# Last stage of an FNet and ReGLU layer: the second column half of B22 made with seven products of quarters, with the sums of weights prepared in the gate stage

## The chip, the cores and the metric

One NeuronCore of a Trainium2 chip runs the whole kernel in one launch. The metric is the device time of the launch in microseconds (us), lower is better; the time before is the median of three runs. Engines are named as in the profile: PE (matrix products), PEld (PE's weight loads), DVE (vector), ACT (scalar), POOL (general, here also a queue of transfers), SP (a queue of transfers).

## The reference

```python
xn = layernorm(x)                                  # x: 1 x 2048 x 640, fp32
a, b = xn @ dft_hid_re.T, xn @ dft_hid_im.T        # 640 x 640 each
mix = dft_seq_re @ a - dft_seq_im @ b              # 2048 x 2048 each
gate, up = xn @ W_gate, xn @ W_up                  # 640 x 1728 each
h = gate * (gate > 0) * up
out = x + mix + h @ W_down                         # W_down: 1728 x 640
```

## The kernel before

**Products in three parts.** All products are of fp32 values held as a rounded high part and a low part. `split` (L199 to L201) makes them: ACT copies the high part (L200), DVE subtracts it for the low part (L201). `mm3` (L202 to L208) makes one product of 128 x 128 weights and 128 x 512 values with three matmuls: high by high (L206), high by low (L207), low by high (L208).

**Stages.** The first stage (0 to about 405 us) does the sequence transform. The gate stage (406 to about 699 us) makes `gate`, `up` and `h` in 13 tiles of 128 columns of F. The last stage (700 us to the end) multiplies the hidden transform and `h` by `dft_hid` and `W_down`, and adds x. Both products of the last stage are one long sum over 12 pairs of blocks: five `hid` pairs from the transform, and seven pairs of tiles of `h`, the last of them odd (a tile and the 64 columns left over). Quads are two such pairs each.

**The gate stage.** A tile is a period of 33 units; a unit is a product of three matmuls, 0.68 us. What happens in a period stands in tables of numbers: products and sums in `STEPS`, the making of weight sums in `SUMS`, `WEIGHTS`, `SPLITS`. Each action is entered with a key, `at(key, f)`, and all are written out in the order of their keys; the engines run them in that order. Actions of a tile that this text speaks of: `seed` (ACT, L1102) copies one PSUM bank into another with a sign, `add_snap` (DVE, L1112) adds a kept copy to a bank, `add_out` (DVE, L1117) takes a bank out, `both` (DVE, L1123) makes a new bank of an old one and a kept one, once per tile, `final` (DVE, L1129) makes `h`. PSUM has eight banks, and a bank that such an action frees is what a later product starts in: the third `add_snap` of a tile after `both` frees the bank that ACT's seed then fills for PE's first product of the next tile. The weight sums `gw` (L1007) are placed by `plan_sums` on DVE or beside it on POOL, by due times; the `w`, `wa`, `wb` instructions (L1083) are the low parts of the sums.

**Tasks.** The gate stage also prepares weights of the last stage. A task has five steps, each with its own key: load on SP (tile `pl`), TASK_LEAD units ahead of the task's key; prepare on DVE (four small sums, `pw`); a rounding on ACT 1.2 units later; `rounded` on DVE (a subtraction of 512 or 384 columns) at the task's second key; the store on SP TASK_STORE later. `pair_half` tasks (24) make the sums for a pair of blocks and write them to `wparts`. `quad_weights` tasks (5) make the sums for a quad of blocks (L1306, L626, L1308, L626, and L1317 for `rounded`), and write to `wquads`. The 29 tasks stand three to a period from period 2, the last two in period 11. `plain_parts` copies go beside them on POOL.

**`grow`.** The products of quarters also need sums of the moving operand. `grow` builds them in memory with POOL's transfers from memory to memory, some of them accumulating: for each of three groups a chain of eight transfers (`grown`), 14 units apart; each link waits for the one it reads.

**The last stage.** `project(q)` runs for the sequence halves q = 1, then q = 0. For each it makes products of sums of halves named B11, T1, T2, B22, B21, T3, T4, over seven `UNITS`. Each unit has load, fetch (weights), prepare (`split`), run and read (additions to the output tile `y`, DVE, L1452 and L1454). B22 is the product that is treated on a second level, for column half 0: `second_level` replaces it with seven products of quarters, named 1256374, over three `GROUPS` (5 blocks in all) and both sequence halves at once. Four of the seven have a second product for an odd row block. Column half 1 of B22 is made straight. `QUADS_AFTER` says after which units of `project` the next of the 21 quarter units comes. `drive_last` runs each unit's load 0, fetch and prepare some steps ahead of its run: AHEAD 6, ROWS 6, READY 3. Weights have seven buffers (`wts`), the split operands four (`ring2`), the loaded operands 16 (`raws`). In this stage PE, SP and POOL are written out by hand, DVE and ACT are ordered by the scheduler.

Of the kernel before, what the change touches and what calls it, by code (L numbers as in the profile page):

```python
# [128 lines left out]
def fnet_reglu_kernel(  # L129
# [42 lines left out]
    wquads = dram_p.tile([P, len(QUADS), 4, 2 * P], F32, name="wquads")  # L172
    grown = [dram_p.tile([4, P, n, CH], F32, name=f"grown{g}") for g, (_, _, n, _) in enumerate(GROUPS)]
# [840 lines left out]
    def plan_sums():  # L1014
# [278 lines left out]
    def quad_weights(i):  # L1293
# [25 lines left out]
        def store():  # L1319
            nc.sync.dma_start(wquads[:, i], t["s"].rearrange("p s v n -> p s (v n)"))  # L1320
# [3 lines left out]
    tasks = [quad_weights(i) for i in range(len(QUADS))] + [pair_half(k, h) for k in range(NPAIR) for h in range(2)]  # L1324
    assert len(tasks) <= len(TASK_KEYS) * (NF - 3)
    for i, (load, prepare, round_, rounded, store) in enumerate(tasks):
        key, second = (PERIOD * (2 + i // len(TASK_KEYS)) + key for key in TASK_KEYS[i % len(TASK_KEYS)])
# [8 lines left out]
    def quarter(q, g, half):  # L1336
        what, k, n, _ = GROUPS[g]
        if what == "hid":
            return pqd[2 * q][1][:, k + half * n : k + half * n + n]
        first = 2 * (k + half * n) + 1  # L1340
        return hd[q][first : first + 2 * n - 1 : 2, :, :CH].rearrange("f p t -> p f t")

    def grow(g):

        t = [grown[g][i] for i in range(4)]
        put = lambda o, i: lambda: nc.gpsimd.dma_start(o, i)
        more = lambda o, i: lambda: nc.gpsimd.dma_start(o, i, accum_op=OP.add)
        return [put(t[0], quarter(1, g, 0)), put(t[2], quarter(0, g, 1)), more(t[0], quarter(0, g, 0)), more(t[2], quarter(0, g, 0)),
                put(t[1], t[0]), more(t[1], quarter(0, g, 1)), put(t[3], t[1]), more(t[3], quarter(1, g, 1))]
# [75 lines left out]
    Y_BEFORE = {(1, "T1", 6): "B11", (1, "T2", 1): "T1"}  # L1425
# [40 lines left out]
    def project(q):  # L1466
# [7 lines left out]
        def get(kind, u):  # L1474
# [5 lines left out]
            col, row = int(kind in ("B12", "B22")), int(kind in ("B21", "B22"))  # L1480
# [13 lines left out]
        def unit(name, u, first, last):  # L1494
# [7 lines left out]
            def load():  # L1502
# [8 lines left out]
                if q and name == "T2" and u in (1, 5):  # L1511
                    get("B21", SINGLE[u // 5])
# [24 lines left out]
            def prepare():  # L1537
# [3 lines left out]
                r = lambda kind: raws[kind, u]  # L1541
# [109 lines left out]
        for name, us in (("B11", every), ("T1", every), ("T2", every), ("B22", every[:4]), ("T3", every), ("B22", every[4:]), ("T4", every)):  # L1651
            for u in us:
                now = [(name, u, u == every[0], u == every[-1])]
# [14 lines left out]
    def second_level():  # L1668
# [132 lines left out]
```

## Time and profile before

| what | value |
|---|---|
| median of three runs | 1001.67 us (1001.63 to 1002.9) |
| profiled execution, whole | 1000.28 us |
| its span | 998.5 us |
| PE busy | 992.9 us, 99% (4393 matmuls) |
| DVE busy | 883.0 us, 88% |
| ACT busy | 525.7 us, 53% |
| POOL busy | 147.0 us, 15% |
| granted clock of PE | 1.00 |
| moved by transfers | 261.13 MB, mean 262 GB/s |

The time of the profiled execution is 1.8 us above its span, and the median of the runs 1.4 above that. A row of the timeline reads: start, duration (both us), engine, line, operation, output<-inputs, shape, and in brackets the idle time of the engine just before with what ended it. A row of the waits reads: who waited, for whom, us in total, times, the longest. A row of groups ends with count, busy us, mean ns, and the idle time before.

### The profile page before, as it was taken

To read this page: it belongs to the slowest core of one execution; us is meant where nothing else is said; L and a number is where in the kernel's file an instruction comes from. 1 tells how busy PE (TensorE), PEld (TensorE's weight loads), DVE (VectorE), ACT (ScalarE), POOL (GpSimd) and SP (SyncE) were. 2 spreads that over 40 slices of the span, in tenths; PEclk is the share of its full clock that TensorE was granted. 3 is DMA by queue.
4 is the path that set the end of the run, shared out by engine and by line. 5 is a ranking of instruction groups with operands and counts; after the bars stand their busy time and mean duration, and the time that the engine had idled before them with its cause. 6 is when DMAs were issued, how large, how long until landed. Compare 5 with 4: busy or idle time off the path is not lost.

```text
span 998.5 us, 13547 instructions
## 1 busy us (share of the span) xinstructions
PE 992.9 (99%) x4393; PEld 818.4 (82%) x4393; DVE 883.0 (88%) x1459; ACT 525.7 (53%) x832; POOL 147.0 (15%) x288
## 2 busy tenths in 40 slices
PE   9999999999999999999999999999999999999998
PEld 8888888888888888878888888888788888888887
DVE  7967999999889989998999999997788887689887
ACT  6664444333333555776666666666444354454452
POOL 2000000000000000024444544432100000000001
PEclk9999999999999999999999999999999999999999
DMA  8977895985947967827997998765698879999784
GB/s 323 322 262 262 261 328 171 342 332 183 408 157 252 361 203 247 289 74 195 276 268 239 259 267 259 207 185 160 202 400 304 261 243 344 312 314 322 230 275 163
DMA packets 183670, 261.13 MB, mean 262 GB/s; under 512 B 14944, under 2 KB 127200, under 8 KB 183504
## 3 DMA queue, kind: packets, MB, share of 16 engines
q1 hardware_dynamic: 147200, 208.82, 61.9%
q0 software_dynamic: 10944, 38.44, 13.0%
q10 hardware_dynamic: 25456, 13.01, 4.4%
q8 instruction: 34, 0.56, 0.2%
q14 instruction: 36, 0.29, 0.1%
HBM read 198.34 MB, written 75.94 MB: 275 GB/s over the span
## 4 chain that ended last, share of the span: by engine, by line
PE 95%; DVE 3%; issue 1%; DMA 1%; ACT 0%; SPq 0%; DVEq 0%; ACTq 0%
PE ps L207 30%; PE ps L206 30%; PE ps L208 30%; PE ps L584 3%; PE ps L613 1%; PE ps L1599 1%; DMA pl<-in_wd 1%; PE ps L185 1%; DVE ev L1117 1%; DVE ev L1129 0%; DVE w L1083 0%; DVE gw L1007 0%; DVE wt L201 0%; DVE ps L1112 0%; DVE pw L1282 0%
## 5 line engine op out<-in xcount | busy, mean ns | idle before, releaser
L208 PE MATMUL ps<-cb,wt 128*128 128x512 f32 (+1 forms) x389 | 151.0, 388 | 0.2 <-DVE wt L201 0.2
L207 PE MATMUL ps<-cb,wt 128*128 128x512 f32 (+1 forms) x389 | 151.0, 388 | 0.1
L206 PE MATMUL ps<-cb,wt 128*128 128x512 f32 (+1 forms) x389 | 150.9, 388 | 0.0
L200 ACT ACTIVATE cb<-rw 128x1024 fp32r<-128x1024 f32 (+1 forms) x91 | 86.5, 962 | 82.5 <-PE ps L208 47.7
L200 ACT ACTIVATE cb<-raw 128x1024 fp32r<-128x1024 f32 x64 | 67.7, 1060 | 103.7 <-PE ps L208 61.8
L201 DVE TENSOR_TENSOR cb<-rw,cb 128x1024 fp32r<-128x1024 f32 (+1 forms) x91 | 99.3, 1103 | 18.7 <-ACT cb L200 17.9
L207 PE MATMUL ps<-cb,xs_late 128*128 128x512 f32 x232 | 90.6, 390 | 0.0
L206 PE MATMUL ps<-cb,xs_late 128*128 128x512 f32 x232 | 90.3, 389 | 0.0
L208 PE MATMUL ps<-cb,xs_late 128*128 128x512 f32 x232 | 90.3, 389 | 0.0
L201 DVE TENSOR_TENSOR cb<-raw,cb 128x1024 fp32r<-128x1024 f32 x64 | 77.9, 1219 | 13.3 <-ACT cb L200 13.2
L1102 ACT ACTIVATE ps<-ps 128x512 f32<-128x512 f32 x104 | 59.2, 581 | 56.3 <-DVE ps L1112 37.2
L207 PE MATMUL ps<-cb,xs_early 128*128 128x512 f32 x226 | 88.0, 390 | 0.0
L206 PE MATMUL ps<-cb,xs_early 128*128 128x512 f32 x226 | 87.9, 389 | 0.0
L208 PE MATMUL ps<-cb,xs_early 128*128 128x512 f32 x226 | 87.9, 389 | 0.0
L197 ACT ACTIVATE ev<-ps 128x512 f32<-128x512 f32 x117 | 70.0, 598 | 33.4 <-PE ps L208 31.6
L207 PEld LDWEIGHTS ps<-cb,wt 128*128 128x128 f32 x389 | 73.0, 188 | 15.6 <-DVE cb L201 0.5
L208 PEld LDWEIGHTS ps<-cb,wt 128*128 128x128 f32 x389 | 73.0, 188 | 15.4 <-DVE wt L201 0.6
L206 PEld LDWEIGHTS ps<-cb,wt 128*128 128x128 f32 x389 | 73.0, 188 | 15.2
L1117 DVE TENSOR_TENSOR ev<-ps,ev 128x512 f32<-128x512 f32 x91 | 62.3, 685 | 11.3 <-PE ps L208 10.4
L200 ACT ACTIVATE wt<-wt 128x768 fp32r<-128x768 f32 (+5 forms) x60 | 38.3, 646 | 51.0 <-DMA wt<-wparts 49.5
L1007 POOL TENSOR_TENSOR gw<-gw 128x128 f32<-128x128 f32 x101 | 47.0, 465 | 95.4 <-DVE wa L1083 25.1
L200 ACT ACTIVATE cb<-tk 128x1024 fp32r<-128x1024 f32 x32 | 33.8, 1060 | 51.0 <-DVE tk L751 25.5
(250 smaller groups left out, 2309.4 us busy)
## 6 DMA issues: line engine op xcount, KB each, us to landing
raw<-in_dft SPq DMA_DIRECT2D x94, 512.0 KB, 6.7
wt<-wparts SPq DMA_DIRECT2D x74, 256.0 KB, 4.6
rw<-hd SPq DMA_DIRECT2D x27, 512.0 KB, 6.1
hd<-ev SPq DMA_DIRECT2D x45, 256.0 KB, 3.8
tok<-r ACTq DMA_DIRECT2D x24, 448.0 KB, 6.3
wt<-wparts SPq DMA_DIRECT2D x27, 384.0 KB, 5.2
rw<-pq SPq DMA_DIRECT2D x19, 512.0 KB, 5.9
wparts<-pw SPq DMA_DIRECT2D x24, 384.0 KB, 4.3
```

Source lines behind the costliest of these rows:

```text
L185: nc.tensor.matmul(ps[:, :P], warm, warm, start=True, stop=True)
L197: return nc.scalar.activation(o, i, AF.Copy)
L200: nc.scalar.activation(hi, src, AF.Copy)
L201: return nc.vector.tensor_tensor(lo, src, hi.bitcast(F32), op=OP.subtract)
L206: nc.tensor.matmul(ps, wh, mh, start=first, stop=False, skip_group_check=more)
L207: nc.tensor.matmul(ps, wh, ml, start=False, stop=False, skip_group_check=more)
L208: nc.tensor.matmul(ps, wl, mh, start=False, stop=last, skip_group_check=more)
L584: nc.tensor.matmul(E[0, key], xn_part(n * SG + j, d)[v == 1], b[:, int(v == 2), j], start=False, stop=n % NH == NH - 1 and (j, v) == (SG - ...
L613: nc.tensor.matmul(E[c, key], xn_part(j, d)[v == 1], b[c][0][:, int(v == 2), j], start=j == 0 and v == 0, stop=False)
L1007: return (engine or nc.vector).tensor_tensor(operand(n, o), operand(n, a), operand(n, b), op=OP.add if op == "+" else OP.subtract)
L1102: nc.scalar.activation(banks[n, x], banks[n, s], AF.Copy, scale=float(sign))
L1117: tt(t, banks[n, x], snaps[n, s], op=OP.add if op == "+" else OP.subtract)
```

## The change

The second level is now used for column half 1 too: `second_level(c)` is run for c = 0 and 1. `project` makes B22 straight only for the two units of `SINGLE` (a pair left over and the odd pair). Column half 1 needs its own sums of weights, so there are five more `quad_weights` tasks, which read `Z4` of `wparts` as `pair_half` tasks have stored it, and its own sums of operands, so `grow` runs twice, the second chain 7 units behind the first. The 34 tasks stand three in period 1, three in each of periods 2 to 10, and four in period 11. The load of a task is 12.2 units ahead instead of 13, and its store 2.2 after the second step instead of 2.8. The due times of `plan_sums` move by some units. The places of the quarter units, of SINGLE's and of the loads of `y` are given anew, and the pool of loaded operands is divided. In the last stage this gives five products (15 matmuls) fewer on PE, 20 more instructions on ACT, and 21 loads of quarters (`rq`) more on SP.

```diff
-TASK_STORE = 2.8
-TASK_LEAD, TASK_KEYS = 13.0, ((8.2, 12.4), (18.6, 22.4), (31.2, 33.1))
-LOAD_LEAD, LOADED, RAW_DUE = 46, 38, 8.5
+TASK_STORE = 2.2
+TASKS_FIRST, TASKS_LAST = ((13.9, 18.9), (21.5, 27.5), (31.2, 33.9)), ((6.0, 9.0), (13.9, 17.5), (22.4, 26.0), (28.2, 34.3))
+TASK_LEAD, TASK_KEYS = 12.2, ((8.2, 11.8), (18.6, 22.4), (30.2, 32.1))
+LOAD_LEAD, LOADED, RAW_DUE = 46, 38, 9.5
...
-                due[i] = min([split_at.get(o, 99.0) - 8, RAW_DUE if raw else 99.0] + [due_at(j) - 0.8 for j in reads.get(o, ())])
+                due[i] = min([split_at.get(o, 99.0) - 5, RAW_DUE if raw else 99.0] + [due_at(j) - 0.8 for j in reads.get(o, ())])
...
-    def quad_weights(i):
+    def quad_weights(i, c):
...
-                nc.sync.dma_start(z[:, j * 2 * P : (j + 1) * 2 * P], pair(k, 1)[1][0][:, : 2 * P])
+                nc.sync.dma_start(z[:, j * 2 * P : (j + 1) * 2 * P], wparts[:, k, Z4 : Z4 + 2 * P] if c else pair(k, 1)[1][0][:, : 2 * P])
...
-    tasks = [quad_weights(i) for i in range(len(QUADS))] + [pair_half(k, h) for k in range(NPAIR) for h in range(2)]
-    assert len(tasks) <= len(TASK_KEYS) * (NF - 3)
+    tasks = [quad_weights(i, 0) for i in range(len(QUADS))] + [pair_half(k, h) for k in range(NPAIR) for h in range(2)]
+    tasks += [quad_weights(i, 1) for i in range(len(QUADS))]
+    keys = {1: TASKS_FIRST, NF - 2: TASKS_LAST}
+    task_at = [(PERIOD * n + a, PERIOD * n + b) for n in range(1, NF - 1) for a, b in keys.get(n, TASK_KEYS)]
...
     for g, key in enumerate((60, 184, 300)):
-        for i, step in enumerate(grow(g)):
-            at(key + 14 * i, step)
+        for c in range(2):
+            for i, step in enumerate(grow(g, c)):
+                at(key + 14 * i + 7 * c, step)
...
-                       ("wts2", AHEAD - 4, "left"), ("raws", 16, "left"),
+                       ("wts2", AHEAD - 4, "left"), ("raws", 9, "left"), ("quad", 5, "left"), ("y3", 1, "left"),
...
-    SINGLE_AFTER = ((("B22", 4), ("B22", 5)), (("B22", 0), ("B22", 1)))
-    QUADS_AFTER = [(1, "B22", u) for u in every[3:]] + [(0, "B11", u) for u in every] + [(0, "T1", u) for u in every[:6]] + [(0, "B22", u) for u in every[:4]]
+    SINGLE_AFTER = ((("T3", 6), ("B22", 4)), (("B22", 2), ("B22", 4)))
+    QUADS_AT = {1: {'T3': (0, 1, 1, 1, 0, 1, 2), 'T4': (0, 2, 1, 1, 2, 1, 1)}, 0: {'B11': (2, 2, 3, 3, 2, 2, 1), 'T1': (1, 0, 0, 2, 0, 2, 1), 'T2': (1, 2, 1, 0, 1, 0, 0), 'B22': (0, 0, 2, 0, 0, 0, 0)}}
...
-        for name, us in (("B11", every), ("T1", every), ("T2", every), ("B22", every[:4]), ("T3", every), ("B22", every[4:]), ("T4", every)):
+        for name, us in (("B11", every), ("T1", every), ("T2", every), ("B22", SINGLE if q else SINGLE[:1]), ("T3", every), ("B22", () if q else SINGLE[1:]), ("T4", every)):
...
-    quads = second_level()
-    Y_AFTER = {(1, "T2", 5): ((4, 0),), (1, "T4", 5): ((0, 0), (1, 0))}
+    quads = second_level(0) + second_level(1)
+    Y_AFTER = {(1, "T2", 5): ((4, 0),), (1, "T3", 2): ((0, 0), (1, 0))}
```

Line numbers in the changed kernel are one higher from L199 to L1300 (L1113 there is L1112 here, L1308 is L1307 and so on, `grow`'s L1346 and L1347 are L1350 and L1351). DVE in the gate stage from `both` of tile 0 (L1123) on, to the first two `add_snap` of the next (L1112); before:

```order
L1123 TENSOR_TENSOR ps<-ev_3731,ps 128x512
L1083 TENSOR_TENSOR wb<-st,wb 128x384
L852 TENSOR_TENSOR r_2757<-r_2757 128x512
L1117 TENSOR_TENSOR ev_3765<-ps,ev_3518 128x512
L1007 TENSOR_TENSOR gw<-gw 128x128
L1083 TENSOR_TENSOR w_3757<-gw,w_3757 128x384
L1007 TENSOR_TENSOR gw<-gw 128x128
L1112 TENSOR_TENSOR ps<-ps,ev_3777 128x512
L1007 TENSOR_TENSOR gw<-gw 128x128
L1112 TENSOR_TENSOR ps<-ps,ev_3548 128x512
```

and now (L1124 is `both`, L1113 `add_snap`):

```order
L1124 TENSOR_TENSOR ps<-ev_3741,ps 128x512
L1307 TENSOR_TENSOR pw<-pl 128x128
L627 SCALAR_TENSOR_TENSOR pw<-pw,pl 128x128
L1309 TENSOR_TENSOR pw<-pl 128x128
L627 SCALAR_TENSOR_TENSOR pw<-pl,pw 128x128
L1084 TENSOR_TENSOR wb<-st,wb 128x384
L853 TENSOR_TENSOR r_2761<-r_2761 128x512
L1118 TENSOR_TENSOR ev_3781<-ps,ev_3522 128x512
L1084 TENSOR_TENSOR w_3773<-gw,w_3773 128x384
L1008 TENSOR_TENSOR gw<-gw 128x128
L1318 TENSOR_TENSOR pw<-pw 128x4x128
L1113 TENSOR_TENSOR ps<-ps,ev_3793 128x512
```

One whole task (`pw`) stands between `both` and the first `add_snap`; a second follows before the third `add_snap`, and a third before the next `both`.

DVE in period 11 from `both` to the first `add_snap`, before, with a `pair_half` task (L1271 to L1275):

```order
L1123 TENSOR_TENSOR ps<-ev_6213,ps 128x512
L1083 TENSOR_TENSOR wb<-st,wb 128x384
L1117 TENSOR_TENSOR ev_6247<-ps,ev_5978 128x512
L1007 TENSOR_TENSOR gw<-gw 128x128
L1083 TENSOR_TENSOR w_6240<-gw,w_6240 128x384
L1271 MEMSET pl 64x256
L1272 TENSOR_TENSOR pw<-pl 128x128
L1273 TENSOR_TENSOR pl<-pl 128x128
L1274 TENSOR_TENSOR pl<-pw,pl 128x128
L1275 TENSOR_TENSOR pw<-pl 128x128
L1007 TENSOR_TENSOR gw<-gw 128x128
L1112 TENSOR_TENSOR ps<-ps,ev_6259 128x512
```

and now, with a `quad_weights` task, whose second step also lies ahead of the `add_snap`:

```order
L1124 TENSOR_TENSOR ps<-ev_6279,ps 128x512
L1307 TENSOR_TENSOR pw<-pl 128x128
L627 SCALAR_TENSOR_TENSOR pw<-pw,pl 128x128
L1309 TENSOR_TENSOR pw<-pl 128x128
L627 SCALAR_TENSOR_TENSOR pw<-pl,pw 128x128
L1084 TENSOR_TENSOR wb<-st,wb 128x384
L1118 TENSOR_TENSOR ev_6320<-ps,ev_6038 128x512
L1084 TENSOR_TENSOR w_6310<-gw,w_6310 128x384
L1318 TENSOR_TENSOR pw<-pw 128x4x128
L1008 TENSOR_TENSOR gw<-gw 128x128
L1113 TENSOR_TENSOR ps<-ps,ev_6333 128x512
```

The task's second step moved ahead of the first `add_snap`; two more prepares (L1307 to L627) and one more second step follow before the third, where one `pair_half` second step stood before.

POOL at the start of the first chain of `grow`, before; the other rows are weight sums (`gw`) and copies to `wparts`:

```order
L1347 DMA grown_98<-pq_88 128x1024
L1007 TENSOR_TENSOR gw<-gw 128x128
L1251 DMA wparts<-in_hid 128x256
L1007 TENSOR_TENSOR gw<-gw,st 128x128 x3
L1251 DMA wparts<-in_hid 128x128
L1007 TENSOR_TENSOR gw<-gw,st 128x128
L1251 DMA wparts<-in_hid 128x256
L1347 DMA grown_98<-pq_88 128x1024
```

and now:

```order
L1351 DMA grown_99<-pq_88 128x1024
L1008 TENSOR_TENSOR gw<-gw 128x128
L1252 DMA wparts<-in_hid 128x256
L1008 TENSOR_TENSOR gw<-gw 128x128
L1008 TENSOR_TENSOR gw<-gw,st 128x128
L1351 DMA grown_102<-pq_89 128x1024
```

A link of the second chain (`grown_102`) now stands between two links of the first.

More of the change, by code (lines that the diff above doesn't have):

```diff
@@ L171, in fnet_reglu_kernel @@
     wparts = dram_p.tile([P, NPAIR, NW], F32, name="wparts")
-    wquads = dram_p.tile([P, len(QUADS), 4, 2 * P], F32, name="wquads")
-    grown = [dram_p.tile([4, P, n, CH], F32, name=f"grown{g}") for g, (_, _, n, _) in enumerate(GROUPS)]
+    wquads = [dram_p.tile([P, len(QUADS), 4, 2 * P], F32, name=f"wquads{c}") for c in range(2)]
+    grown = [[dram_p.tile([4, P, n, CH], F32, name=f"grown{c}{g}") for g, (_, _, n, _) in enumerate(GROUPS)] for c in range(2)]
     nc.vector.memset(eps_t, EPS)
@@ L1439, in fnet_reglu_kernel @@
     for at, n in {(1, 0): 2, (1, 1): 1, (1, 4): 1, (0, 0): 2, (0, 1): 2, (0, 4): 2}.items():
-        missing[at + (0,)] += n
+        for c in range(2):
+            missing[at + (c,)] += n
     missing[0, 3, 0] += 2
@@ L1444, in get_y @@
         for e, c in which:
-            own = f"{q}" if e in (0, 1, 4) and c == 0 else ""
+            own = f"{q}" if e in (0, 1, 4) else ""
             y[q, e, c] = t = pool(Y_AT[f"{e}{c}{own}"]).tile([P, CH], F32, name=f"y{e}{c}{own}")
@@ L1479, in get @@
                 o = raws[kind, u] = (in_turns("lead") if kind == "B11" else in_turns("low") if kind == "B12" else pool("raws")).tile([P, 2, CH], F32, name="rw")[:, : len(ks)]
-            col, row = int(kind in ("B12", "B22")), int(kind in ("B21", "B22"))
+            col, row = int(kind in ("B12", "B22")), int(kind in ("B21", "B22", "own"))
             if what == "odd":
@@ L1511, in load @@
                 if q and name == "T2" and u in (1, 5):
-                    get("B21", SINGLE[u // 5])
+                    get(*(("B21", ODD_AT) if u == 5 else ("own", SINGLE[0])))
             def fetch():
@@ L1540, in prepare @@
                 sub = lambda o, i0, i1: nc.vector.tensor_tensor(o, i0, i1, op=OP.subtract)
-                r = lambda kind: raws[kind, u]
+                r = lambda kind: raws["own" if (q, kind, name, u) == (1, "B21", "B21", SINGLE[0]) else kind, u]
                 if short:
@@ L1650, in project @@
         steps = []
[L1651 removed]
+        for name, us in (("B11", every), ("T1", every), ("T2", every), ("B22", SINGLE if q else SINGLE[:1]), ("T3", every), ("B22", () if q else SINGLE[1:]), ("T4", every)):
             for u in us:
[L1653 removed]
+                ends_at = SINGLE if name == "B22" else every
+                now = [(name, u, u == ends_at[0], u == ends_at[-1])]
                 for at, single in zip(SINGLE_AFTER[q], SINGLE):
@@ L1679, in unit @@
             odd = name in ("1", "2", "5", "3")
-            src = {"1": quarter(1, g, 0), "2": quarter(1, g, 1), "3": quarter(0, g, 1)}.get(name)
-            src = grown[g][{"5": 0, "6": 1, "7": 2, "4": 3}[name]] if src is None else src
+            src = {"1": quarter(1, g, 0, c), "2": quarter(1, g, 1, c), "3": quarter(0, g, 1, c)}.get(name)
+            src = grown[c][g][{"5": 0, "6": 1, "7": 2, "4": 3}[name]] if src is None else src
             def load():
-                t["r"] = pool("raws").tile([P, 2, CH], F32, name="rw")[:, :n]
+                t["r"] = pool("quad").tile([P, 2, CH], F32, name="rq")[:, :n]
                 nc.sync.dma_start(t["r"], src)
@@ L1691, in fetch @@
                 if part is not None:
-                    put(w[:, :, : 2 * P], wquads[:, at : at + n, part])
+                    put(w[:, :, : 2 * P], wquads[c][:, at : at + n, part])
                     if odd:
                         put(w[:, :, 3 * P : 4 * P], own[:, :, O2 : O2 + P])
+                elif odd and c:
+                    put(w[:, :, 2 * P : 3 * P], own[:, :, O2 : O2 + P])
+                    put(w[:, :, 3 * P : 4 * P], own[:, :, Z4 : Z4 + P])
                 elif odd:
@@ L1757, in fnet_reglu_kernel @@
                 todo.append(alone((lambda which: lambda: get_y(0, *which))(Y_AFTER[of])))
-            if of in QUADS_AFTER:
+            for _ in range(QUADS_AT[of[0]].get(of[1], (0,) * len(UNITS))[of[2]]):
                 todo.append(quads.pop(0))
```

31 lines of the change are left out of this document (17 added, 14 removed).

## The prediction

> **What bounds the kernel now.** I read the page first: the share of each engine, then the chain that ended last.
>
> ```profile
> span 998.5 us, 13547 instructions
> PE 992.9 (99%) x4393; PEld 818.4 (82%) x4393; DVE 883.0 (88%) x1459; ACT 525.7 (53%) x832; POOL 147.0 (15%) x288
> PE 95%; DVE 3%; issue 1%; DMA 1%; ACT 0%; SPq 0%; DVEq 0%; ACTq 0%
> ```
>
> PE (the matmul engine) is busy 99% of the span and carries 95% of the chain. So a matmul that goes away is worth its whole pitch, and any wait of PE that arises is paid whole. DVE, at 88%, is the next engine that could take over. The second view was PE's waits in the gate and last stages, 400 to 999 us, and the third busy time by stretches (columns: PE, PEld, DVE, ACT, POOL, granted clock, DMA share, GB/s).
>
> ```profile
> PE ps L206 <- DVE ps L1123: 0.3, 1, 0.3
> PE ps L208 <- DVE wt L201: 0.2, 1, 0.2
> 428.55:451.10 22.55, 22.55 (x100) 18.17 (x99) 21.73 (x46) 17.44 (x36) 6.93 (x15) 1.00 0.28 92
> 654.05:676.60 22.55, 22.39 (x99) 18.21 (x98) 21.35 (x51) 14.84 (x30) 7.92 (x17) 1.00 0.55 150
> 532.00:603.00 71.00, 71.00 (x314) 58.59 (x313) 67.15 (x164) 47.17 (x96) 34.03 (x66) 1.00 0.92 257
> 738.00:750.00 12.00, 12.00 (x55) 9.94 (x54) 11.90 (x14) 7.04 (x9) 0.00 (x0) 1.00 1.06 400
> 750.00:950.00 200.00, 199.84 (x882) 165.15 (x881) 164.58 (x196) 95.70 (x124) 4.86 (x9) 1.00 0.87 291
> 695.00:999.00 304.00, 299.21 (x1322) 246.81 (x1320) 246.37 (x299) 139.53 (x185) 11.36 (x21) 1.00 0.83 279
> ```
>
> The reader is to see that PE's waits are one by one a few tenths, that DVE is busy about 95% of the two gate periods that get more tasks (first two window rows), and that the DMA engines are already at 0.92 of their time in the third. The granted clock is 1.00 throughout, so the clock is no term.
>
> **Matmuls removed.** The ten blocks of the second column half of B22 by three row blocks by two sequence halves were 60 products; the seven quarter products are 35 and, for the odd row block, 20. Five products fewer, each three matmuls: 15. One matmul is worth the distance between starts, not its 0.39 us:
>
> ```profile
> 448.65 0.69 DVE L1112 TENSOR_TENSOR ps<-ps,ev 128x512 f32<-128x512 f32 x1
> 449.38 0.58 ACT L1102 ACTIVATE ps<-ps 128x512 f32<-128x512 f32 x1 [2.50 <-DVE ps L1112]
> 449.94 0.39 PE L206 MATMUL ps<-r,w 128*128 128x512 f32 x1
> ...
> 450.62 0.39 PE L206 MATMUL ps<-r,wa 128*128 128x512 f32 x1
> ```
>
> From 449.94 to 450.62 are three pitches, 0.227 each; 15 make **-3.4 us**.
>
> **Three more tasks in period 1.** These rows are also the chain that period 1 hangs on: DVE's third add of the tile (448.65), which frees ACT's seed (449.38 to 449.96, after ACT had sat idle 2.50 us for it), which PE's first product of the next tile needs (450.62). Its slack is about 0.6 us (450.62 less 449.96, and a little for the signal). In the changed order two whole tasks and the prepare of a third come between `both` of tile 0 and `both` of tile 1, the first two ahead of this add. What a task costs DVE:
>
> ```profile
> 438.13 0.69 DVE L1123 TENSOR_TENSOR ps<-ev,ps 128x512 f32<-128x512 f32 x1
> 439.59 0.69 DVE L852 TENSOR_TENSOR r<-r 128x512 fp32r<-128x512 f32 x1 [0.30 <-ACT r L844]
> ...
> 453.94 0.68 DVE L1129 SCALAR_TENSOR_TENSOR ev<-ev,ev 128x512 f32<-128x512 f32 x1
> 454.54 0.28 DVE L1306 TENSOR_TENSOR pw<-pl 128x128 f32<-128x128 f32 x1
> ...
> 455.47 0.49 DVE L1007 TENSOR_TENSOR gw<-gw 128x128 f32<-128x128 f32 x2
> 458.91 0.68 DVE L1317 TENSOR_TENSOR pw<-pw 128x512 f32<-128x512 f32 x1
> ```
>
> The four prepare instructions take 454.54 to 455.47, 0.93; the wide subtraction has the 0.68 of the row at 453.94, after which the next starts 0.60 later. So 1.53 a task, 3.06 for two, less one 0.2 sum that POOL now takes. DVE's idle time between 438.13 and 448.65 that can swallow some is the 0.30 at 439.59 and some 0.2 in smaller gaps. The add comes some 2.35 later, the slack of 0.6 is used, and PE stands **+1.7** (bounds: 0, if the tables' other sums leave room; 2.4, if no idle is swallowed). A second reading agrees: DVE's instructions from `both` to `both`, at pitches of 0.60, 0.47 and 0.20 for 512, 384 and 128 columns, were 18.9 and become 23.2 in a period that PE needs 22.5 for. The later periods have 20.3 again, so this is paid once.
>
> **Four tasks instead of two in period 11.** The same chain two hundred microseconds on:
>
> ```profile
> 662.72 0.69 DVE L1123 TENSOR_TENSOR ps<-ev,ps 128x512 f32<-128x512 f32 x1
> 664.57 0.69 DVE L1117 TENSOR_TENSOR ev<-ps,ev 128x512 f32<-128x512 f32 x1 [0.44 <-PE ps L208]
> 674.22 0.69 DVE L1112 TENSOR_TENSOR ps<-ps,ev 128x512 f32<-128x512 f32 x1
> 674.94 0.58 ACT L1102 ACTIVATE ps<-ps 128x512 f32<-128x512 f32 x1 [3.43 <-DVE ps L1112]
> 675.58 0.50 PE L206 MATMUL ps<-r,wa 128*128 128x512 f32 x1 [0.16 <-ACT ps L1102]
> ```
>
> Here the slack is gone already: PE waits 0.16. From 662.72 to the add at 674.22 DVE has 10.2 us of work by pitches before and 12.0 after (three prepares and two subtractions instead of one task of the older kind and three sums). Of the 1.8 more, the idle 0.44 and some tenths are swallowed: the add is 1.2 late, and PE loses **+1.1** (bounds 0.6 and 1.8). The changed times of tasks in the other periods leave 9.6 to 10.0 us in that stretch, as before, and cost nothing.
>
> **The last stage.** DVE does there, per changed product, the splits and additions of these rows (count, busy, mean ns; the last is a row of DVE's timeline):
>
> ```profile
> L201 DVE TENSOR_TENSOR cb<-rw,cb 128x1024 fp32r<-128x1024 f32 x71 | 86.1, 1221 | 17.7 <-ACT cb L200 17.0
> L1452 DVE TENSOR_TENSOR y<-ps,y 128x512 f32<-128x512 f32 x41 | 26.5, 683 | 4.7 <-PE ps L208 4.6
> L201 DVE TENSOR_TENSOR wt<-wt 128x768 fp32r<-128x768 f32 x27 | 25.6, 954 | 13.4 <-ACT wt L200 13.4
> L201 DVE TENSOR_TENSOR cb<-rw,cb 128x512 fp32r<-128x512 f32 x20 | 13.7, 686 | 1.0 <-ACT cb L200 0.9
> L201 DVE TENSOR_TENSOR wt<-wt 128x256 fp32r<-128x256 f32 x8 | 3.4, 419 | 0.8 <-ACT wt L200 0.8
> L201 DVE TENSOR_TENSOR wt<-wt 128x512 fp32r<-128x512 f32 x4 | 2.7, 687 | 0.0
> L201 DVE TENSOR_TENSOR wt<-wt 128x128 fp32r<-128x128 f32 x3 | 0.9, 284 | 0.0
> 986.38 2.52 DVE L201 TENSOR_TENSOR cb<-rw,cb 128x1024 fp32r<-128x1024 f32 x2
> ```
>
> The change has 4 more of the first, 10 more additions, 10 fewer of the third, 7 more of the fourth, then 8, 4 and 3 more: 4.9 + 6.8 - 9.5 + 4.8 + 3.4 + 2.7 + 0.9 = 13.9 us. DVE goes from 246.4 of 304 to 260.3 of 300.6, 87%. That is still cover, but the products of quarters are spread over stretches in which the buffers (seven of weights, four of split operands) cover less time each. In the tail, T3 and T4 of the first sequence half, DVE is still splitting at 986.38 to 988.90, ten microseconds from the end (last row), so it is only a little ahead of PE. I take **+0.3**, near the lower bound 0, since PE's only wait there is the 0.2 for `wt`; the upper bound 2.5 is a sixth of the work added.
>
> Transfers there: 42 loads of quarter operands instead of 21, 12 more of prepared weights, and the smaller ones, less the straight loads; 10.4 MB more by their sizes, over about 190 us. The row of 750 to 950 then goes from 291 to some 345 GB/s, and the row at 738 shows 400 with PE busy throughout. I count nothing.
>
> The Trainium skill, "DMA: Bandwidth & Descriptors", section "Specifications", puts the limit of the memory at about 358 GB/s for a core. This trace shows 400 in a stretch of 12 us, so the measurement decides and I don't use it; by the rule the sum would have the third rival's price in it.
>
> **Transfers of the gate stage.** The five more tasks load ahead by 12.2 units instead of 13 (8.3 us by 33 units in 22.5 us), and POOL's accumulating chains are doubled: 24 more transfers, one every 7 units, each link of a chain still 14 units (9.5 us) after the one before.
>
> ```profile
> DMA to landing us min/median/max: 2.5/4.5/9.4
> grown<-hd POOLq DMA_DIRECT2D x5, 512.0 KB, 8.8
> q0 software_dynamic: 1965, 5.60, 35.6%
> ```
>
> First row: the task loads (`pl`), 430 to 700 us; their median is half of their lead. Second: a link of the chain (530 to 586) lands in 8.8, inside its 9.5. The third, of the window 532 to 603, gives the price of POOL's queue there: 5.60 MB in 35.6% of 71 us, 4.5 us of all engines per MB. The second chain brings 4.2 MB more, 19 us or 0.27, upon 0.92. That can't all fit at that price; but 400 GB/s were moved at 1.06 and here 257, so the price shrinks when the queue is fuller. Late links delay only the next links, POOL's sums behind them, and loads that have 6 to 7 us to spare. I take 0 (bounds 0 and +4), and this is the weakest term.
>
> **Sum.** -3.4 + 1.7 + 1.1 + 0.3 = -0.3. The profiled execution took 1000.28, of which 998.5 is span; the median of the runs is 1001.67, 1.4 above it. On the median: **1001.4**.
>
> **Rivals.** *The saving stays whole.* DVE's lateness in periods 1 and 11 is swallowed by idle time that I counted as needed: its lower busy share in period 1 by pitches (18.9 of 22.5) speaks for it; the 0.16 that PE already waits in period 11, and 23.2 us of work in a period of 22.5, against. At most -3.4: 998.3.
>
> *The gate stage's transfers come late.* Place: the stretches of the second and first chain, 471 to 519 and 556 to 603. It decides where a task's load lands later than about 7 us after its issue (the longest now is 9.4, so it has happened), or a link later than 9.5, so that POOL's sums and DVE's prepares stand in order behind it. Some ten tasks lie in the two chains; at 0.4 to 0.8 lost for each that is late beyond the slack, +4 on the sum: 1005.4, slower. For it: 0.92 + 0.27. Against: loads and chain are spread, and a normal load lands in half its lead.
>
> *The last stage becomes bound.* By DVE in the tail (87%, and little ahead of PE), or by transfers that cannot go much faster than the 291 of the long row: a stretch that needs 375 GB/s, of which two of 24 us come in the first half's T1 and T2, would take 2.3 us more at a ceiling of 358 than at 400. +2.3: 1003.7. By the skill's rule this would be the case; the row of 400 GB/s speaks against.
>
> **Chances.** Forecast 0.47, saving whole 0.18, late transfers 0.22, last stage bound 0.13. What differs by 0.2% (2.0 us) is about what a measurement of this kernel can tell from no change. Faster by that: most of the first rival and a little of the forecast's spread, 0.22. Slower: the late transfers nearly whole, half of the last rival, a little of the forecast, 0.31. Same: 0.47. The range reaches from the saving whole to the late transfers: 998.4 to 1005.6; the forecast's own is 1000 to 1003.
>
> **What would show it.** PE should have 4378 matmuls; a wait for ACT's L1102 or DVE near 451 us of 1 to 2 us and another of about 1 near 675; DVE about 260 us in the last stage with no wait of PE above some tenths. I am wrong if these two waits are absent (then the saving shows), if waits for `gw` or `w` appear between 470 and 603 with `pl` landing in 7 us or more, or if PE waits for `cb` or `wt` in the last stage by more than 1 us.

## The result, and the profile after

The changed kernel takes 1026.88 us (median of four runs, 1025.61 to 1030.32) against 1001.65 before: ratio 1.0256, interval 1.0242 to 1.027, so 25 us slower. The matmuls did go, 4393 to 4378. The page of the profiled execution, 1030.32 us:

```profile
span 1028.5 us, 13766 instructions
PE 1002.5 (97%) x4378; PEld 815.5 (79%) x4378; DVE 906.4 (88%) x1510; ACT 534.1 (52%) x853; POOL 165.6 (16%) x312
PE 53%; DVE 21%; DMA 11%; issue 11%; ACT 2%; POOL 1%; SPq 1%; DVEq 0%; ACTq 0%; POOLq 0%
```

PE carried 95% of the chain and now carries 53%; DVE, transfers and issues carry the rest. PE's waits over the whole span, then three gate windows and one of the last stage (columns as in the prediction), then the three gate windows of the kernel before:

```profile
PE ps L207 <- ACT ps L1103: 11.4, 9, 4.5
PE ps L208 <- DVE cb L202: 3.4, 4, 1.2
PE ps L207 <- DVE ev L1118: 3.2, 2, 2.9
```

```profile
471.00:495.00 24.00, 21.06 (x92) 17.04 (x91) 19.66 (x46) 13.56 (x28) 11.52 (x22) 1.00 1.04 282
495.00:519.00 24.00, 23.81 (x98) 19.17 (x98) 21.21 (x52) 14.24 (x30) 11.70 (x23) 0.93 0.90 241
556.00:580.00 24.00, 19.49 (x87) 15.82 (x86) 18.34 (x45) 12.43 (x25) 9.58 (x17) 1.00 0.97 266
850.00:875.00 25.00, 24.50 (x107) 19.73 (x106) 19.84 (x23) 13.51 (x17) 1.08 (x2) 1.00 1.05 377
```

```profile
471.00:495.00 24.00, 24.00 (x107) 19.89 (x106) 22.74 (x55) 15.51 (x31) 11.16 (x23) 1.00 0.97 292
495.00:519.00 24.00, 24.00 (x107) 19.86 (x107) 22.52 (x57) 15.83 (x33) 11.42 (x23) 1.00 0.88 245
556.00:580.00 24.00, 24.00 (x107) 19.82 (x107) 22.81 (x57) 15.66 (x33) 11.42 (x23) 1.00 0.95 264
```

The big losses stand in the gate stage, where the transfer engines are busy for 0.90 to 1.04 of their time and move 241 to 282 GB/s. That alone doesn't mark the loss: the kernel before has 0.88 to 0.97 at 245 to 292 GB/s in the same windows, with PE busy throughout. The engines move about as much per us, and the new transfers come on top. In the last stage 377 GB/s were moved with PE nearly busy, so the limit of about 358 GB/s for a core that the Trainium skill states ("DMA: Bandwidth & Descriptors", section "Specifications") was no ceiling here either.

Where the time goes is best read from one instruction that stands once in each tile: `both` on DVE. The table gives how much later it starts than in the kernel before, in us, worked out from the timeline rows of each kernel. The columns right of "changed" are experiments told below. They are one execution each, and not always one near the median: that of the changed kernel is the slowest of its four, 3.4 us above the median, and that of the two chains in the kernel before ended 5 us ahead of its run's median.

| tile | before starts at | changed | one chain | before, two chains | old tasks | last stage alone | chain moved |
|---|---|---|---|---|---|---|---|
| 0 | 438.13 | 3.4 | 1.6 | -0.2 | 1.6 | 0.0 | 2.2 |
| 1 | 460.34 | 5.2 | 3.5 | -0.2 | 1.6 | 0.0 | 4.0 |
| 2 | 482.78 | 5.6 | 3.5 | -0.1 | 1.6 | 0.0 | 4.3 |
| 3 | 505.22 | 10.7 | 4.9 | 0.3 | 4.4 | 0.3 | 6.4 |
| 5 | 550.14 | 11.8 | 5.0 | 1.2 | 6.1 | 0.3 | 6.4 |
| 6 | 572.63 | 18.8 | 5.0 | 7.4 | 11.2 | 0.2 | 6.4 |
| 8 | 617.60 | 24.6 | 5.2 | 14.0 | 18.6 | 0.2 | 6.5 |
| 10 | 662.72 | 24.8 | 5.7 | 13.7 | 18.3 | 0.2 | 9.2 |
| 12 | 708.05 | 27.0 | 7.3 | 13.7 | 18.3 | 0.2 | 11.8 |
| end of span | 998.5 | 30.0 | 10.3 | 13.7 | 21.6 | 2.7 | 14.2 |

In the changed kernel some 19 us come between tiles 2 and 8, 1.8 between tiles 0 and 1, 2.2 after tile 10, and 3.0 in the last stage, which was forecast to gain 3.4 less 0.3. (Up to 2 us of the lateness at tile 0 arises before the gate stage, in waits of the first stage that differ between executions.)

The largest single wait of the changed kernel, rows of POOL, DVE, ACT and PE in order of time:

```profile
562.67 1.08 POOL L1351 DMA_DIRECT2D grown<-hd  x1
...
573.52 1.05 POOL L1351 DMA_DIRECT2D grown<-hd  x1 [5.81 <-issue]
575.08 0.29 DVE L1008 TENSOR_TENSOR gw<-gw,st 128x128 f32<-128x128 f32 x1 [4.51 <-POOL gw L1008]
578.01 0.69 DVE L1113 TENSOR_TENSOR ps<-ps,ev 128x512 f32<-128x512 f32 x1
578.74 0.58 ACT L1103 ACTIVATE ps<-ps 128x512 f32<-128x512 f32 x1 [7.78 <-DVE ps L1113]
579.38 0.50 PE L207 MATMUL ps<-r,wa 128*128 128x512 f32 x1 [4.51 <-ACT ps L1103]
```

POOL stands 5.81 us at the issue of an adding transfer of the chains. The weight sums behind it on POOL come late, DVE waits 4.51 for one, so its add is late, then ACT's seed, and PE stands 4.51. POOL's stands at such issues in all, before and after:

```profile
POOL grown L1347 <- issue: 0.8, 4, 0.3
```

```profile
POOL grown L1351 <- issue: 17.3, 8, 5.8
```

The other large wait has another way in: a store of `hd` lands late, and DVE waits for the buffer `ev` that it reads. SP meanwhile takes 7.11 us to issue two loads:

```profile
488.34 7.11 SPq L1264 DMA_DIRECT2D pl<-in_hid  x2
493.65 0.69 DVE L1118 TENSOR_TENSOR ev<-ps,ev 128x512 f32<-128x512 f32 x1 [4.00 <-DMA hd<-ev]
494.39 0.50 PE L207 MATMUL ps<-mv,wa 128*128 128x512 f32 x1 [2.94 <-DVE ev L1118]
...
496.39 0.63 PE L209 MATMUL ps<-xs_early,w 128*128 128x512 f32 x1
496.81 0.63 PE L207 MATMUL ps<-r,wb 128*128 128x512 f32 x1
```

```profile
DMA to landing us min/median/max: 2.1/5.6/13.8
```

The last row is that of the task loads `pl`, 400 to 725 us: 13.8 us at the worst instead of 9.4, in the median 5.6 instead of 4.5.

### The profile page after: what moved, and what is told of

Read it like the earlier page. It is cut to its first block, busy times and chain, and to the rows that moved or that the text cites. A ratio compares the mean times of both kernels' runs of the same rounds, so it can differ in the third digit from the quotient of the medians.

```text
span 1028.5 us, 13766 instructions
## 1 busy us (share of the span) xinstructions
PE 1002.5 (97%) x4378; PEld 815.5 (79%) x4378; DVE 906.4 (88%) x1510; ACT 534.1 (52%) x853; POOL 165.6 (16%) x312
## 4 chain that ended last, share of the span: by engine, by line
PE 53%; DVE 21%; DMA 11%; issue 11%; ACT 2%; POOL 1%; SPq 1%; DVEq 0%; ACTq 0%; POOLq 0%
PE ps L207 17%; PE ps L208 17%; PE ps L209 17%; DVE cb L202 3%; DMA raw<-in_dft 3%; PE ps L585 3%; DMA pl<-in_hid 2%; DVE ps L1113 2%; DVE gw L1008 1%; DVE raw L752 1%; DVE ev L1118 1%; DVE w L1084 1%; DMA pl<-in_wd 1%; DMA pq<-sa 1%; DMA pl<-wparts 1%
## 5 line engine op out<-in xcount | busy, mean ns | idle before, releaser
L208 PE MATMUL ps<-cb,wt 128*128 128x512 f32 x384 | 149.8, 390 | 2.7 <-DVE cb L202 2.7
L207 PE MATMUL ps<-cb,wt 128*128 128x512 f32 x384 | 149.5, 389 | 0.8 <-DVE y L1460 0.4
L209 PE MATMUL ps<-cb,wt 128*128 128x512 f32 x384 | 149.1, 388 | 0.0
L201 ACT ACTIVATE cb<-rw 128x1024 fp32r<-128x1024 f32 (+1 forms) x60 | 57.2, 965 | 76.4 <-DVE rw L1548 54.8
L208 PEld LDWEIGHTS ps<-cb,wt 128*128 128x128 f32 x384 | 72.1, 188 | 19.9 <-DVE cb L202 5.2
L207 PEld LDWEIGHTS ps<-cb,wt 128*128 128x128 f32 x384 | 72.1, 188 | 17.4 <-DVE y L1460 1.3
L209 PEld LDWEIGHTS ps<-cb,wt 128*128 128x128 f32 x384 | 72.1, 188 | 14.6
L202 DVE TENSOR_TENSOR cb<-rw,cb 128x1024 fp32r<-128x1024 f32 (+1 forms) x60 | 65.4, 1106 | 8.9 <-ACT cb L201 8.3
L1008 POOL TENSOR_TENSOR gw<-gw 128x128 f32<-128x128 f32 x101 | 49.2, 487 | 87.2 <-DVE wa L1084 18.1
L207 PE MATMUL ps<-mv,w 128*128 128x512 f32 x143 | 56.4, 395 | 0.0
```

The source lines that it names most:

```text
L201: nc.scalar.activation(hi, src, AF.Copy)
L202: return nc.vector.tensor_tensor(lo, src, hi.bitcast(F32), op=OP.subtract)
L207: nc.tensor.matmul(ps, wh, mh, start=first, stop=False, skip_group_check=more)
L208: nc.tensor.matmul(ps, wh, ml, start=False, stop=False, skip_group_check=more)
L209: nc.tensor.matmul(ps, wl, mh, start=False, stop=last, skip_group_check=more)
L1008: return (engine or nc.vector).tensor_tensor(operand(n, o), operand(n, a), operand(n, b), op=OP.add if op == "+" else OP.subtract)
```

## The experiments

Times are medians; the ratio is to the kernel before on the same chip. Theory A: the second chain of `grow`. Theory B: the new tasks.

**One chain.** `e1_one_chain`:

```diff
-        for c in range(2):
+        for c in range(1):
...
-            src = grown[c][g][{"5": 0, "6": 1, "7": 2, "4": 3}[name]] if src is None else src
+            src = grown[0][g][{"5": 0, "6": 1, "7": 2, "4": 3}[name]] if src is None else src
```

> The changed kernel with one chain of grow: the 24 transfers of the second chain are left out, and the quarters of column half 1 take the first chain's sums; all else, the five new tasks included, is as changed. Theory A (the second chain fills the transfer engines in the gate stage, so stores of hd and loads of pl land late): most of the 19 us that periods 2 to 8 lost come back, about 1007 us (1004 to 1011), and no wait of PE above 1.5 us in the gate stage. Theory B (the tasks and their shorter lead are what is late): 1024 to 1027.

Measured 1011.53 (1.0095, 1.008 to 1.0111). 15.3 us come back, which ends just outside theory A's interval (at most 1011) and far from theory B; the gate stage's waits for the seed shrink to

```profile
PE ps L207 <- ACT ps L1103: 3.1, 3, 1.1
```

**Two chains in the kernel before.** `e2_before_two_chains`, the loop over `c` of the change, put into the kernel before:

```diff
-        for i, step in enumerate(grow(g)):
-            at(key + 14 * i, step)
+        for c in range(2):
+            for i, step in enumerate(grow(g, c)):
+                at(key + 14 * i + 7 * c, step)
```

> The kernel before with the second chain of grow added in the gate stage, 7 units behind the first; nobody reads its sums. Theory A: the lateness of periods 2 to 8 comes up here too, 1016 to 1022 us. Theory B: 1001 to 1003, as before. Between them (1006 to 1012): the chain alone is half of it, and the tasks' loads or the shorter lead the rest.

Measured 1018.78 (1.0179, 1.0158 to 1.02): the chain alone costs 17 us, with nobody reading what it makes. Its largest wait is the one of the changed kernel again, POOL, DVE and PE:

```profile
562.32 1.05 POOL L1347 DMA_DIRECT2D grown<-hd  x1 [4.88 <-issue]
564.29 0.49 DVE L1007 TENSOR_TENSOR gw<-gw 128x128 f32<-128x128 f32 x2 [3.99 <-POOL gw L1007]
567.80 0.80 PE L206 MATMUL ps<-r,wa 128*128 128x512 f32 x1 [3.67 <-ACT ps L1102]
```

The price isn't spread evenly. By the table, 12.8 of the 13.7 us of this execution come between tiles 5 and 8, with the middle group. By tile 5, after the first group's chains, only 1.2 are lost, although the transfer engines are full there; PE is busy throughout this window:

```profile
471.00:495.00 24.00, 24.00 (x108) 19.79 (x107) 22.58 (x54) 15.18 (x30) 13.09 (x25) 1.00 1.05 322
```

Why the middle group costs more here, no run shows. The four executions of this run lie 8 us apart (1014.03 to 1021.96), so the place of the loss need not be the same in each.

**The tasks of before.** `e3_old_tasks` (five tasks fewer, all numbers as before):

```diff
-    tasks += [quad_weights(i, 1) for i in range(len(QUADS))]
...
-                    put(w[:, :, : 2 * P], wquads[c][:, at : at + n, part])
+                    put(w[:, :, : 2 * P], wquads[0][:, at : at + n, part])
```

> The changed kernel with the tasks, leads and due times of the kernel before: the five new tasks are left out, and column half 1 takes the prepared weights of column half 0. Both chains stay. Theory A: only what the new tasks cost in periods 1 and 11 comes back (1.8 and 2.2 us in the trace), and perhaps the 3.4 ahead of them: 1019 to 1024. Theory B: 1002 to 1006.

Measured 1021.33 (1.02, 1.0182 to 1.0218): theory B is out as the main cause; the tasks with their numbers (keys, leads, due times) are worth 5.5 beside two chains.

**The last stage alone.** `e4_last_stage_only`, the edits of `e1_one_chain` and `e3_old_tasks` together.

> Neither the new tasks nor the second chain: the gate stage is that of the kernel before, the last stage that of the changed one (its column half 1 takes the sums of half 0). It shows what the last stage is worth by itself. By the trace of the changed kernel, 30.0 us late at the end, 27.0 at the last tile: the last stage pays 3.4 in matmuls and loses 6.4, so 1004 to 1005. If those losses came from the late gate stage, the 15 matmuls show: 998 to 1000.

Measured 1004.32 (1.0027, 1.0018 to 1.0037). So the 15 matmuls don't pay even without any cost in the gate stage. The parts: 2.9 here, 7.2 for the tasks with their numbers (1011.5 less 1004.3), 15.3 for the chain beside them, together the 25. In this run's last stage PE waits and stretched starts take 7.0 us from 700 us on, against 1.3 before (sum of what each distance between successive starts has above 0.227); 5.7 lost, 3.4 won. The waits for `cb`, and the rows of the largest, ACT and PE, and of the last one:

```profile
PE ps L208 <- DVE cb L202: 2.4, 3, 1.2
```

```profile
778.78 2.19 ACT L201 ACTIVATE cb<-rw 128x1024 fp32r<-128x1024 f32 x2 [4.40 <-DVE rw L1545]
781.59 0.50 PE L208 MATMUL ps<-cb,wt 128*128 128x512 f32 x1 [1.20 <-DVE cb L202]
991.90 0.50 PE L208 MATMUL ps<-cb,wt 128*128 128x512 f32 x1 [0.97 <-DVE cb L202]
```

ACT idles 4.40 us until DVE has made a sum of operands (`rw`), DVE then still owes the low part, and PE stands. DVE is in one piece of work from 772 to 792 there. In the kernel before it is busy 19.7 of these 20 us too, without making PE late by more than 0.3, so DVE had no slack to give there before the change either.

The chain's price could lie in POOL's queue (theory C) or in the transfer engines (theory D). **More room in POOL's queue**, `e5_ring`:

```diff
-    nc = bacc.Bacc("TRN2", target_bir_lowering=False, num_devices=1, dynamic_dma_scratch_size=1024)
+    nc = bacc.Bacc("TRN2", target_bir_lowering=False, num_devices=1, dynamic_dma_scratch_size=1536)
```

> The changed kernel with half as much again of room for the descriptors of POOL's transfers (1536 bytes instead of 1024). In the runs so far POOL stands 15 to 17 us in eight issues of accumulating transfers, its weight sums stand behind them, DVE waits for the sums, then ACT's seed and PE. Theory C (POOL stands because its own queue has no room until older transfers have gone): the stands go down to a few us and most of the 17 us that the second chain costs come back, 1010 to 1016 us. Theory D (the 16 transfer engines are full; room in the queue changes nothing, or lets POOL's transfers crowd out the others): 1023 to 1030.

Measured 1021.75 (1.0207, 1.018 to 1.0233), between the ranges of the two theories. POOL's stands are nearly gone, so they were a matter of room:

```profile
POOL grown L1351 <- issue: 1.5, 6, 0.4
```

The time is not gone with them: only 5 of 15.

**Half the pieces**, `e6_merged`, the middle group's two chains as one, with rows of 4 KB:

```diff
-        for c in range(2):
+        for c in range(2) if g != 1 else (None,):
```

> The changed kernel with the two chains of the middle group (two pairs of tiles of h) made one: each of its eight transfers takes both column halves, 4 KB in a row instead of 2 KB, so the same bytes in half the pieces and half the issues. The other two groups keep their two chains. Theory C (pieces and issues of POOL's queue): the lateness of periods 5 to 8, 12.8 us in the changed kernel, falls to 0 to 3, so 1013 to 1018. Theory D (bytes on full engines): 1023 to 1028.

Measured 1021.79 (1.0205, 1.0183 to 1.0227), between again; periods 5 to 8 lose 7.5 instead of 12.8.

**Copies instead of additions**, `e7_plain_second`, on the kernel before:

```diff
-        more = lambda o, i: lambda: nc.gpsimd.dma_start(o, i, accum_op=OP.add)
+        more = lambda o, i: lambda: nc.gpsimd.dma_start(o, i, accum_op=OP.add) if c == 0 else nc.gpsimd.dma_start(o, i)
```

> The kernel before with the second chain, whose transfers copy instead of adding (its sums aren't made, and nobody reads them); as many transfers, rows and waits as in the run with the adding chain, 1018.8 us. If adding is what makes POOL's queue slow: 1002 to 1007. If pieces and issues alone count, or the bytes written: 1014 to 1020.

Measured 1003.85 (1.0023, 1.0012 to 1.0033): 2.3 instead of 17. Of the chain's 24 transfers 12 add, and it is these additions that cost. POOL's queue between 447 and 610 us in the kernel before, then the queue and POOL's stands with copies, then both with additions (the run with two chains):

```profile
q0 software_dynamic: 3936, 12.26, 33.5%
```

```profile
q0 software_dynamic: 5562, 19.92, 45.0%
```

```profile
POOL grown L1347 <- issue: 3.0, 7, 1.3
```

```profile
q0 software_dynamic: 5567, 18.68, 49.0%
```

```profile
POOL grown L1347 <- issue: 16.5, 8, 4.9
```

As many packets, and more bytes, in less of the engines' time with copies. An estimate from these rows, with the first chain's price taken as unchanged and the run with additions later in its work: the second chain takes 2.4 us of all engines per MB with copies and 3.9 with additions, where the queue took 4.5 before.

A full set of engines is not the price by itself, and neither are late loads. With copies the engines are as full, at a higher rate (0.99 of their time at 305 GB/s from 471 to 603 us, against 1.00 at 284 with additions), and the task loads land as late (10.6 us at the worst, against 10.3). What differs most in this pair is POOL's stand at its issues.

**Room, in the kernel before**, `e9_ring_two_chains`, the room of 1536 with two adding chains.

> The kernel before with the second adding chain (1018.8 us) and 1536 bytes of room for POOL's descriptors instead of 1024. In the changed kernel the room took POOL's stands away but only 5 us off the time. If the room is all that the second chain lacks where the tasks are those of before: 1002 to 1006. If the engines' fullness is as much of it: 1009 to 1013 (half of the 17 us left).

Measured 1017.21 (1.0155, 1.0128 to 1.0183), above both expectations: the intervals with and without the room overlap. POOL's stands, DVE's second longest wait for a task's load, and the landing of those loads:

```profile
POOL grown L1347 <- issue: 1.6, 7, 0.4
DVE pw L1306 <- DMA pl<-in_wd: 5.3, 1, 5.3
```

```profile
DMA to landing us min/median/max: 2.4/6.2/14.1
```

With room, POOL issues four adding transfers between 467 and 478 us, and the task loads of 476.9 land at 491, 14 us later; PE stands 3.71 for it. The wait has moved from POOL to SP's loads. The Trainium skill, "DMA: Bandwidth & Descriptors", section "Issuing engines are not separate DMA queues", says that transfers of all issuing engines end up on the same 16 transfer engines and interleave there; this trace agrees, as SP's loads land at 14 us beside POOL's additions.

**Both remedies**, `e11_merged_ring`, and **loads 16 units ahead** with the room, `e12_lead`:

```diff
-TASK_LEAD, TASK_KEYS = 12.2, ((8.2, 11.8), (18.6, 22.4), (30.2, 32.1))
+TASK_LEAD, TASK_KEYS = 16.0, ((8.2, 11.8), (18.6, 22.4), (30.2, 32.1))
```

> The changed kernel with both remedies, the merged chain of the middle group and the room of 1536 (1021.8 us each alone). If they cure the same thing (POOL's queue): 1019 to 1022. If pieces on the engines are a second thing: 1014 to 1018.

> The changed kernel with the room of 1536 (1021.8 us) and the tasks' loads 16 units ahead instead of 12.2. There DVE waited 8.8 us for late loads of tasks. If the lead is what is missing now: 1012 to 1016. If full engines make everything late, stores of hd too: 1019 to 1023.

Measured 1027.06 (1.0262, 1.0247 to 1.0276) and 1021.05 (1.0188, 1.0169 to 1.0208). The first is worse than either remedy by itself, which neither expectation had; the second changes nothing. So it isn't one queue or one lead. In the first, DVE's longest wait is 7.8 us, for a transfer, and PE's is 6.6, for the seed. Theory C explains the stands, and room is worth 5 of the 15 us in the changed kernel, but most of the time stays when the stands go. What is left stands in transfers that land late (theory D); that the additions crowd the others out is inferred from these rows, not tested by itself.

**The chain moved to where the engines have room**, `e13_moved` in the changed kernel and `e14_before_moved` in the one before:

```diff
-                at(key + 14 * i + 7 * c, step)
+                at((key + 14 * i, (4 + 14 * i, 307 + 14 * i, 384 + 7 * i)[g])[c], step)
```

> The changed kernel with the second chain moved to where the transfer engines have room before the change: the group of the transform at keys 4 to 102 (from 409 us), the middle group at 307 to 405 (from 614 us), the last at 384 to 433. Same transfers, same adding. Theory D (adding transfers on engines that are full between 471 and 603 us crowd out stores and loads, or stand in POOL's queue): most of the 17 us come back, 1011 to 1016. If a second adding chain costs its price wherever it stands: 1022 to 1028.

> The kernel before with the second chain in the same moved places (1018.8 us with it 7 units behind the first). Theory D: 1002 to 1006. If it costs its price anywhere: 1013 to 1020.

Measured 1017.14 (1.0163, 1.0147 to 1.018) and 1007.32 (1.0062, 1.0047 to 1.0077): 10 and 11 us come back with the same transfers, a little short of what was expected. Before the change the transfer engines are busy for 0.53 of their time from 409 to 471 us and 0.70 from 614 to 680, against 0.92 from 471 to 603. Of what the moved chain still costs, most arises late, after tile 8 (table, against the run with one chain): links now stand close at the end of the gate stage, and POOL waits for the link before:

```profile
POOL grown L1351 <- DMA grown<-grown: 8.3, 2, 5.9
```

**Copies in the changed kernel**, `e16_after_plain`, the edit of the copies above.

> The changed kernel whose second chain copies instead of adding (column half 1's sums are not made). If adding is what costs here too: 2 to 3 us above the run with one chain, 1013 to 1015. If copies cost as much beside the earlier and denser tasks: 1022 to 1027.

Measured 1015.91 (1.0145, 1.0129 to 1.016): 11 of the 15 us are the adding; 4.4 stay, more than the 2.3 of the kernel before. The tasks stand earlier and denser here, which may be why; no run tests it.

**Due times**, `e15_due`, on the run with one chain:

```diff
-LOAD_LEAD, LOADED, RAW_DUE = 46, 38, 9.5
+LOAD_LEAD, LOADED, RAW_DUE = 46, 38, 8.5
...
-                due[i] = min([split_at.get(o, 99.0) - 5, RAW_DUE if raw else 99.0] + [due_at(j) - 0.8 for j in reads.get(o, ())])
+                due[i] = min([split_at.get(o, 99.0) - 8, RAW_DUE if raw else 99.0] + [due_at(j) - 0.8 for j in reads.get(o, ())])
```

> The run with one chain and the new tasks (1011.5 us) with the due times of the weight sums as before (8 units ahead of the split instead of 5, raw ones at 8.5 instead of 9.5). If the wait of 1.0 us at 429 us, and the 0.3 to 0.4 around it, come from the changed due times, they go: 1009.5 to 1010.5. If from elsewhere: 1011 to 1012. If the later due times were what made room for the tasks: 1013 or more.

Measured 1008.44 (1.0073, 1.0058 to 1.0088): 3.1 of the tasks' 7.2 are the changed due times, more than expected, though the two intervals overlap. The wait at 429 us (431.07 in the changed kernel) is gone.

**Fewer columns in ten additions**, `e8_small_adds`, and **another place for an odd unit**, `e10_order`, both on the last stage alone:

```diff
-                    add_y(q, e, c, ps, op=op)
+                    add_y(q, e, c, ps, op=op, cols=32 if c else CH)
```

```diff
-    SINGLE_AFTER = ((("T3", 6), ("B22", 4)), (("B22", 2), ("B22", 4)))
+    SINGLE_AFTER = ((("T3", 6), ("B22", 4)), (("B22", 2), ("T3", 1)))
```

> The run with the last stage alone (1004.3 us) with the ten additions to y of column half 1's quarter products done on 32 of 512 columns: about 0.5 us of DVE saved in each, 5 in all, PE, transfers and order otherwise as there. If the stage's lost 6 us are DVE being late by amount of work: 1000.5 to 1002.5. If they come from the order alone or from transfers: 1004 to 1005.

> The run with the last stage alone (1004.3 us) with one unit elsewhere: for q = 1 the odd unit of B21 runs after T3's second unit instead of right behind B22's odd unit, so that the two odd units, short on PE and long on DVE, no longer stand together. If the 2.3 us that PE loses in two places at 770 to 790 us of that run come from this order: 1001.5 to 1003, and no wait of PE for cb there. If from the amount of DVE's work or from transfers: 1004 to 1005, the wait elsewhere.

Measured 1003.06 (1.0011, 1.0002 to 1.0019) and 1004.73 (1.0035, 1.0021 to 1.0048). The first lies just above what was expected if the amount of DVE's work were all; its wait at 780 us stays. In the second that wait shrinks from 1.20 to 0.29, and two more come behind it, one of them for an ACT copy:

```profile
PE ps L207 <- ACT cb L201: 1.5, 1, 1.5
```

So in the last stage it is DVE's amount of work around 780 us and in the tail, rather than the place of one unit. That is an inference from two small differences; the 5.7 us are not taken apart further.

**The moved chain with the due times of before**, `e17_moved_due` (middle group 17 units apart, last from key 391), complete in what it computes.

> The changed kernel, complete in what it computes, with both remedies: the second chain moved (the middle group's links 17 units apart instead of 14, the last group from key 391 on) and the due times of the weight sums as before. If the two parts add up: 1017.1 less 3.1 for the due times, less up to 2 for POOL's stands at the end, 1012 to 1014 us. If the later due times are what the moved chain needs on POOL: 1016 to 1018. It stays above the kernel before in either case, by the tasks (4) and the last stage (3).

Measured 1014.42 (1.0127, 1.011 to 1.0144): just above the sum, 12.5 us better than the change and 13 above the kernel before. No version here beats the kernel before.

## Why the prediction was wrong

The result lies far above the forecast and above every rival (the dearest was 1005.4). The account by the terms of the sum:

**Matmuls, -3.4: right.** 15 fewer, and the span of the run with the last stage alone is 2.7 longer, of which 5.7 are lost and 0.2 arose earlier: about -3.2.

**Three tasks in period 1, +1.7: right.** From tile 0 to tile 1 the changed kernel loses 1.8, the run with one chain 1.8, the runs with the old tasks none. With the due times of before it is 2.0. **Period 11, +1.1: too small.** 2.2, and 1.6 with one chain. Both terms show as waits for ACT's seed, as worked out (second and third row); the first row is a wait that the prediction did not have:

```profile
431.07 0.50 PE L207 MATMUL ps<-r,wa 128*128 128x512 f32 x1 [0.97 <-ACT ps L1103]
455.70 0.50 PE L207 MATMUL ps<-r,wa 128*128 128x512 f32 x1 [0.97 <-ACT ps L1103]
702.58 0.50 PE L207 MATMUL ps<-r,wa 128*128 128x512 f32 x1 [1.09 <-ACT ps L1103]
```

**Due times, priced at nothing because not looked at:** 3.1. In the tile ahead of the first new task the add that the seed waits for comes 7.9 us after the add before it instead of 6.8, with another order of weight sums on DVE and 0.82 us of waiting for ACT between them. Of the change's numbers the prediction followed those of the tasks and not this one.

**The last stage, +0.3 with 2.5 as the upper bound: wrong by 5.4.** The step that failed is taking a value near the lower bound because PE had nearly no waits there before. 5.7 us came out. Much of it stands where DVE had no slack for more work (its share by stage, 87%, says nothing of 772 to 792 us); that this is all of it is inferred.

**Transfers of the gate stage, 0 with +4 as the upper bound: wrong by 15 to 17, and this decides.** The sum of engine time was there: 0.92 and 0.27 more. The step that failed is "the price shrinks when the queue is fuller", taken from 400 GB/s in the last stage. There SP loads tiles; here POOL adds in memory. By the estimate above the price shrank for copies (4.5 to 2.4 us per MB) and much less for additions (3.9), and in time the chain cost 2.3 us as copies and 17 with additions. The rival was named with the right place and the right waits (POOL's sums, task loads), and these signs of being wrong came up. Its price was too low: 0.4 to 0.8 for each of some ten tasks is 4 to 8, of which the prediction took 4, and it let each late load cost its own lateness. It was 3 to 5 us at a time (4.51, 3.67, 2.94), since a late sum on POOL holds up DVE, and what stands behind that sum on DVE comes late with it.

## What to carry to other kernels

Where a queue's own price per byte says that a stretch will not fit (0.92 + 0.27), believe it until a row of the same kind of transfer shows a lower one; rows of another kind do not. Look at a transfer's kind and place before its size: the chain cost 17 us with additions in one place, 6 with them moved to stretches where the engines were less busy, and 2 as copies in the first place. A late transfer costs what stands in order behind it, not its own lateness. A saving of PE time needs to be set against the slack of the next engine in the very microseconds where its work lands.

## What was not expected of the hardware

After PE had stood 2.94 us (row of 494.39), its matmuls started 0.42 apart instead of 0.227 (496.39, 496.81), until 498.10; the granted clock from 494.39 to 498.10 is 0.55. The lower rate of those nine starts cost another 1.7 us (3.71 less nine times 0.227). In the run with the chain moved in the kernel before, a stand of 2.67 us (at 651.60) left the clock at 1.00. The prediction had said that the clock is no term. The Trainium skill, "TensorE: Matmul & The Clock Gate", Part 1, says that PE falls to half rate after an idle window of about 3.4 us and stays there until about 3.4 us of work; the trace agrees in the rate and in the time of slow work, 3.4 us after the wait of 4.51 us (580.2 to 583.6) and 3.7 here, but the idle time here was a little shorter than that window.

An adding transfer costs POOL itself more than a copy: in the run with copies, one of the first chain's additions and one of the second chain's copies, of the same size, stand side by side:

```profile
564.97 1.13 POOL L1347 DMA_DIRECT2D grown<-hd  x1
569.38 0.69 POOL L1347 DMA_DIRECT2D grown<-hd  x1 [1.26 <-issue]
```

The addition takes 1.13 us to issue, the copy 0.69; with 1024 bytes of room POOL stood up to 5.8 us before one. What inside the transfer engines makes adding slow, no run here shows.
